# Row-sum reciprocals by block transpose and memory instead of TensorE transposes, and last keys over 128 rows

## The chip, the cores and the metric

One core of a Trainium2 chip. Time is device time in microseconds (us). TensorE (PE) multiplies and writes to PSUM, VectorE (DVE) and ScalarE (ACT) read PSUM and SBUF, GpSimd (POOL) works on SBUF, and SyncE's queue (SP) issues every DMA of this kernel. Each engine takes its own list of instructions in order.

## The reference

Causal attention with a decay for 4 x 8 heads of 576 tokens and 64 dimensions, then a mixture of 8 experts over 2304 tokens with iterated normalization of the gate, then a two-layer network:

```python
cum = np.cumsum(np.log(np.clip(f, 0.0001, 1.0)), axis=-1)
scores = scale * q @ k.T + cum[:, None] - cum[None, :]       # per head, causal
attn = np.exp(scores - scores.max(-1, keepdims=True))
x = attn / (attn.sum(-1, keepdims=True) + 1e-09) @ v
P = np.exp(x @ w_gate - max)                                 # then 8 times:
P /= P.sum(1, keepdims=True); P /= P.sum(0, keepdims=True); P *= N / E
y = sum(P[:, e:e+1] * (np.maximum(x @ w1[e], 0) @ w2[e]) for e in range(8))
out = np.maximum(0.01 * (y @ w_in), y @ w_in) @ w_out
```

## The kernel before

**Attention, 0 to 296 us.** Heads are taken one after another and normalized in pairs (even head n with n + 1). For a head, `qk` computes scores in six pieces x over query blocks of 128, 128, 128, 96 and 96 rows (`QKS`), each as two products (L452, L453); `qk_min` (L464, VectorE) masks them and takes the row minimum of the negated scores; `qk_exp` (L477, ScalarE) exponentiates and sums each row into `st`. `tr` (L504, PE) transposes the exponentials, `tr_hi` (L511, ScalarE) copies them out. In most heads the transposed exponentials and v are split into a high and a low part of reduced precision: `tr_lo` (L520, VectorE) makes the low part `ptl`, `vp` and `vl` those of v, and `pv` (L541, PE) multiplies both. `pv` gives the output transposed, dimensions on partitions, tokens along the row, in two column ranges r of 256 and 320 tokens. Keys come in five blocks, the last of which has 64 keys, so its products contract over 64 rows. The heads in `NATIVE` (0, 1, 2, 4 and 6) are not split; their products run in full precision, which takes PE longer. `pv_copy` (ScalarE) and `pv_add` (L569, VectorE) bring the output into `xs`, 128 partitions for two heads.

**Normalization of a pair.** Row sums lie with tokens on partitions, while the outputs have tokens along the row. `recip` (L583 to L585, VectorE) takes reciprocals in `st`; `spread` (L590, GpSimd) copies each 64 times along the row into `rb`; `norm_t` (L599, PE) transposes the five blocks of `rb` into the PSUM tile `ps_r`, blocks 0 and 1, then 2 to 4; `norm_m` (L605, VectorE) multiplies `xs` by it. Then `x_hi`, `x_lo` split `xs`, `x_store` writes it to memory, `gate` (L650, PE) multiplies it by the gate's weights.

**Fills.** Between these PE runs "fills", products of the first experts (L213: 384 columns, L240: 512 columns), with their weights loaded (`wr`, L143) and split (L154, L158). What attention has not taken of the fills follows behind the gate's logits (L944), over the eight normalizations of the gate, and partly between the first expert products (L1400).

**What sets the order.** `head_events` names each step with its engine, an assumed duration, its needs and a due time (tables `HEAD_T`, `HEAD_E` for native heads, `PAIR_T`, `PAIR_E`; `base_of` gives the pace). `run_heads` simulates the five queues with them and writes each engine's list: the earliest start wins, and a later step with an earlier due time may go first within a bound. Fills go in where PE has nothing due. "VP" marks steps of VectorE that are kept apart from GpSimd's. `run_events` does the same for the expert stages, beginning with the fills that are left.

Of the kernel before, what the change touches and what calls it, by code (L numbers as in the profile page):

```python
# [15 lines left out]
ALU = mybir.AluOpType  # L16
# [36 lines left out]
    qk0=0.082, qk1=0.116, qk2=0.397, qk3=0.562, qk4=0.212, qk5=0.672,  # L53
    t0=1.293, t1=1.192, t2=1.370, t3=0.995, pv0=1.618, pv1=1.989,
# [3 lines left out]
    nt0=3.799, ga0=4.707, nt1=3.866, ga1=4.635,  # L58
# [4 lines left out]
NATIVE = (0, 1, 2, 4, 6)  # L63
# [3 lines left out]
    qk0=-0.150, qk1=-0.138, qk2=0.915, qk3=0.306, qk4=0.749, qk5=0.774,  # L67
    t0=1.579, t1=1.706, t2=1.194, t3=0.921, pv0=1.375, pv1=2.127,
)
PAIR_E = dict(  # L70
    nt0=3.970, ga0=4.804, nt1=3.484, ga1=4.601,
# [17 lines left out]
def moe_kernel(ctx, tc, qT, kT, v, fg, w_gate, w1, w2, w_in, w_out, out):  # L89
# [214 lines left out]
    with ExitStack() as actx:  # L304
# [49 lines left out]
        fone = a1.tile([P, 512], F32, tag="p3", name="fone")[:B * H, 0:S // 2]  # L354
# [10 lines left out]
        ca = a2.tile([P, PTW], F32R, tag="pth", name="pth")[:B * H, 0:2 * S].rearrange(  # L365
# [59 lines left out]

        vps = {}
# [13 lines left out]
        QKS = [(4, 0, 288), (4, 288, 576), (0, 0, 128), (1, 0, 256), (2, 0, 384), (3, 0, 512)]  # L440
# [30 lines left out]
        def qk_exp(n, x):  # L471
            i, k0, k9 = QKS[x]
            m = QT[i][1]
            if (n, i) not in prb:
                prb[n, i] = (a2 if i == 4 else a1).tile([P, QN[i]], F32, tag=f"p{i}", name=f"p{i}")
# [16 lines left out]
        def tr(n, u):  # L492
            if n in NATIVE:
                if n not in pts:
                    pts[n] = (a2.tile([P, PTW], F32, tag="pth", name="pt"),)
            elif n not in pts:
                pts[n] = (a2.tile([P, PTW], F32R, tag="pth", name="pth"),
                          a2.tile([P, PTW], F32R, tag="ptl", name="ptl"))
# [28 lines left out]
        def pv(n, r):  # L527
# [5 lines left out]
            for x, (j, s) in enumerate(todo):  # L533
# [3 lines left out]
                if n in NATIVE:  # L537
                    vp = rvs[(n // 2) % 2][:KV[j], j].rearrange("p h d -> p (h d)")
# [35 lines left out]
        rbs, rps, parts = {}, {}, {}  # L574

        def stat(n):
            stats[n // 2] = a2.tile([P, 3, 5, 2], F32, tag="st", name="st")
            nc.gpsimd.memset(stats[n // 2], 1.0)

        def recip(n):  # L580
# [4 lines left out]
            nc.vector.reciprocal(rs, rs)  # L585

        def spread(n):
            rs = stats[n // 2][:, 0]
            rbs[n] = a1.tile([P, 5, P], F32, tag="rb", name="rb")
            nc.gpsimd.tensor_copy(  # L590
                rbs[n].rearrange("p i (h d) -> p (i h) d", h=2),
                rs.rearrange("p i h -> p (i h)").unsqueeze(2).to_broadcast([P, 10, D]))

        def norm_t(n, r):
            ra, rb = RG[r]
            ps = ps_t.tile([P, 512], F32, tag="t", name="ps_r")
            for i in ((0, 1), (2, 3, 4))[r]:
                q0, m = QT[i]
                nc.tensor.transpose(ps[:, q0 - ra:q0 - ra + m], rbs[n][:m, i, :], ident[:m, :m])  # L599
            rps[n, r] = ps  # L600

        def norm_m(n, r):
            ra, rb = RG[r]
            xs = xss[n // 2]
            nc.vector.tensor_tensor(xs[:, ra:rb], xs[:, ra:rb], rps.pop((n, r))[:, :rb - ra], ALU.mult)  # L605
# [63 lines left out]
        TE, TL = 6.9, 8.6  # L669
# [25 lines left out]
        M_QK = (0.27, 0.27, 0.18, 0.235, 0.36, 0.47)  # L695
        M_TR = (0.41, 0.40, 0.48, 0.16)
        V_MN = (0.40, 0.57, 0.22, 0.35, 0.49, 0.65)
        A_EX = (0.47, 0.47, 0.36, 0.46, 0.57, 0.68)
        A_HI = (0.47, 0.44, 0.50, 0.28)
        V_LO = (0.58, 0.55, 0.62, 0.36)  # L700

# [1201 lines left out]
```

## Time and profile before

| | us |
|---|---|
| median of 3 runs | 2006.63 |
| lowest, highest | 2006.27, 2008.97 |
| profiled execution, its own time | 2007.51 |
| its span, first to last instruction | 2005.6 |

| engine | busy us | share |
|---|---|---|
| PE | 1982.9 | 99% |
| VectorE | 1663.2 | 83% |
| ScalarE | 982.7 | 49% |
| GpSimd | 1039.3 | 52% |

Busy PE is not PE at its peak: matmuls overlap, and their ends are modelled. The distance between the starts of two matmuls in the timeline tells what one costs.

### The profile page before, as it was taken

Reading aid. Unit: us, or ns where it says so; the run is one execution under the profiler, and the core shown is the slowest. Engines: PE = TensorE matmul, PEld = TensorE weight load, DVE = VectorE, ACT = ScalarE, POOL = GpSimd, SP = SyncE. Lnnn points to the kernel's source line nnn. Section 1 sums busy time; section 2 is a strip of 40 time slices with the busy share of each in tenths; the row PEclk is TensorE's granted clock in tenths of the full one; section 3 lists DMA queues with packets and bytes.
Section 4 is the critical chain, followed back from the end, with each engine's and each line's share of the span. In section 5 each row is a group of like instructions: output and inputs, shape, how many; then the busy total and the mean of one; then the engine's idle time right before and its main releaser. Section 6 shows DMA issues by size and latency. Waiting matters only on the chain.

```text
span 2005.6 us, 32286 instructions
## 1 busy us (share of the span) xinstructions
PE 1982.9 (99%) x11600; PEld 1941.2 (97%) x11600; DVE 1663.2 (83%) x2467; ACT 982.7 (49%) x1753; POOL 1039.3 (52%) x732
## 2 busy tenths in 40 slices
PE   7999999999999999999999999999999999999999
PEld 6888888999999999999999999999999999999998
DVE  8988976788888888888888888888888878887766
ACT  7877865454433443444344334434433346655443
POOL 5766655345555555555554555555464563343301
PEclk9999999999999999999999999999999999999999
DMA  5655528578887778776777777677777745776563
GB/s 155 185 151 164 142 88 276 200 287 268 277 275 284 260 239 275 246 250 242 254 247 245 272 243 250 241 258 251 243 269 242 249 181 199 276 248 214 194 204 138
DMA packets 145623, 460.55 MB, mean 230 GB/s; under 512 B 15912, under 2 KB 42168, under 8 KB 145464
## 3 DMA queue, kind: packets, MB, share of 16 engines
q1 hardware_dynamic: 145464, 458.49, 68.1%
q8 instruction: 93, 1.52, 0.3%
q14 instruction: 66, 0.54, 0.1%
HBM read 402.76 MB, written 51.08 MB: 226 GB/s over the span
## 4 chain that ended last, share of the span: by engine, by line
PE 91%; DVE 3%; ACT 2%; DMA 2%; issue 1%; SPq 0%; POOL 0%; DVEq 0%; ACTq 0%
PE x L1400 46%; PE y L1400 34%; PE ps_t L504 1%; PE ps_pv L541 1%; DMA wr<-in_w_dram 1%; PE ps_m L240 1%; PE ps_s L452 1%; PE ps_m L213 1%; PE ps_s L453 1%; ACT p L477 1%; PE ps_m L541 1%; PE y L213 1%; PE x L240 1%; DVE ps_s L464 1%; PE x L213 1%
## 5 line engine op out<-in xcount | busy, mean ns | idle before, releaser
L1400 PE MATMUL x<-xw,w 128*128 128x384 f32 x2676 | 499.9, 334 | 0.0
L1400 PE MATMUL x<-hh,w 128*128 128x384 f32 x1792 | 490.6, 334 | 0.0
L1400 PEld LDWEIGHTS x<-xw,w 128*128 128x128 f32 x2676 | 467.2, 188 | 0.7 <-issue 0.3
L1400 PE MATMUL y<-xw,w 128*128 128x384 f32 x2004 | 374.7, 334 | 0.0
L1400 PE MATMUL y<-hh,w 128*128 128x384 f32 x1344 | 368.0, 334 | 0.2 <-DVE acc_C L1483 0.2
L1400 PEld LDWEIGHTS y<-xw,w 128*128 128x128 f32 x2004 | 349.6, 188 | 0.1
L1222 POOL TENSOR_TENSOR w<-wr,w 128x512 fp32r<-128x512 f32 x163 | 211.0, 1295 | 228.0 <-DVE hl L1471 51.6
L1400 PEld LDWEIGHTS x<-hh,w 128*128 128x128 f32 x1792 | 326.8, 188 | 0.0
L1400 PE MATMUL x<-hl,w 128*128 128x384 f32 x896 | 299.4, 334 | 0.3 <-POOL hl L1471 0.3
L1400 PEld LDWEIGHTS y<-hh,w 128*128 128x128 f32 x1344 | 244.9, 188 | 0.5 <-issue 0.5
L1400 PE MATMUL y<-hl,w 128*128 128x384 f32 x672 | 224.5, 334 | 0.0
L1483 DVE TENSOR_TENSOR acc_C<-x,acc_C 128x768 f32<-128x768 f32 x177 | 168.9, 954 | 55.3 <-PE x L1400 52.5
L1483 DVE TENSOR_TENSOR acc_C<-y,acc_C 128x768 f32<-128x768 f32 x148 | 141.5, 956 | 67.1 <-PE y L1400 65.6
L154 ACT ACTIVATE w<-wr 128x512 fp32r<-128x512 f32 x288 | 175.1, 621 | 32.0 <-PE y L1400 15.9
L1400 PEld LDWEIGHTS x<-hl,w 128*128 128x128 f32 x896 | 168.2, 188 | 0.6 <-POOL hl L1471 0.6
L1467 ACT ACTIVATE hh<-u 128x768 fp32r<-128x768 f32 x91 | 77.1, 847 | 151.6 <-PE y L1400 91.2
L1467 ACT ACTIVATE hh<-k 128x768 fp32r<-128x768 f32 x112 | 94.9, 848 | 100.8 <-PE y L1400 50.7
L1467 ACT ACTIVATE hh<-spare 128x768 fp32r<-128x768 f32 x84 | 71.2, 847 | 142.3 <-PE y L1400 65.0
L1400 PEld LDWEIGHTS y<-hl,w 128*128 128x128 f32 x672 | 126.2, 188 | 0.0
L1467 ACT ACTIVATE hh<-c 128x768 fp32r<-128x768 f32 x70 | 59.3, 847 | 118.0 <-PE y L1400 93.5
L1436 ACT ACTIVATE u<-x 128x768 f32<-128x768 f32 x91 | 74.1, 814 | 86.8 <-PE x L1400 80.2
L1210 POOL TENSOR_TENSOR wr<-wr 128x512 f32<-128x512 f32 x55 | 71.2, 1295 | 84.0 <-DVE wr L1210 32.2
(263 smaller groups left out, 3637.2 us busy)
## 6 DMA issues: line engine op xcount, KB each, us to landing
xw<-xo_t SPq DMA_DIRECT2D x208, 768.0 KB
xw<-xo_b SPq DMA_DIRECT2D x154, 768.0 KB
wr<-in_w_dram SPq DMA_DIRECT2D x88, 512.0 KB
pb<-prow SPq DMA_DIRECT2D x44, 384.0 KB
xo_t<-xw SPq DMA_DIRECT2D x16, 768.0 KB
rq<-in_qT_dram SPq DMA_DIRECT2D x64, 144.0 KB
rk<-in_kT_dram SPq DMA_DIRECT2D x64, 144.0 KB
xo_b<-xw SPq DMA_DIRECT2D x12, 768.0 KB
```

The lines of the kernel that those rows point to most:

```text
L154: nc.scalar.activation(hv, src, AF.Copy)
L213: nc.tensor.matmul(ps, w_[:, fs], x_[k][:, xs], start=(x == 0), stop=(x == 11))
L240: nc.tensor.matmul(ps, h_[:, ts], w_, start=(x == 0), stop=(x == 11))
L452: nc.tensor.matmul(o, q1[:, q0:q0 + m], k1[:, k0:k9], start=True, stop=False)
L453: nc.tensor.matmul(o, q2[0:D + 4, q0:q0 + m], k2[0:D + 4, k0:k9], start=False, stop=True)
L541: nc.tensor.matmul(ps[:, a - ra:rb - ra], vp, s[:KV[j], o:o + rb - a], start=(x == 0), stop=(x == len(todo) - 1))
L1210: ENG[e].tensor_tensor(o, x, y, op)
L1222: ENG[e].tensor_tensor(lo, blk(g, which, WSRC[which][n]), f(hi), ALU.subtract)
L1400: nc.tensor.matmul(o_, w[:, k, w_], m[:, k, :], start=a and k + y == 0, stop=z and k == 1 and y == 2, skip_group_check=True)
L1436: nc.scalar.activation(ctile(u, name, name, bufs), pview(u, p), AF.Copy)
L1467: nc.scalar.activation(hi, tmp[u, LSRC[l]], AF.Copy)
L1483: nc.vector.tensor_tensor(a, pview(u, l), a, ALU.add)
```

## The change

The five reciprocal blocks are no longer spread and transposed on PE. `st` becomes 32 columns wide, of which ten hold the sums; VectorE's block transpose turns it in blocks of 32 x 32 into `turned`; four small DMAs write ten rows each to a DRAM tile `rd`, and two DMAs read it back broadcast over 64 partitions each into `rb`, from where `norm_m` multiplies in SBUF, in ranges of 384 and 192 tokens. Heads 3, 5 and 7 become native. The tiles of transposed exponentials are now fixed ones, whose rows beyond the last 64 keys are cleared once, so that the last keys' products run over 128 rows. The last query block computes 480 score columns instead of 512. Due times and assumed durations change (one line of each is shown).

```diff
-    nt0=3.799, ga0=4.707, nt1=3.866, ga1=4.635,
+    nt0=5.002, ga0=4.901, nt1=3.561, ga1=4.607,
...
-NATIVE = (0, 1, 2, 4, 6)
+NATIVE = (0, 1, 2, 3, 4, 5, 6, 7)
...
+        for t_ in [f(t_) for t_ in pths + ptls] + ptfs:
+            nc.gpsimd.memset(t_[D:, PTOFF[4]:], 0.0)
...
+        nc.gpsimd.memset(p3[:, 480:], 0.0)
...
-        QKS = [(4, 0, 288), (4, 288, 576), (0, 0, 128), (1, 0, 256), (2, 0, 384), (3, 0, 512)]
+        QKS = [(4, 0, 288), (4, 288, 576), (0, 0, 128), (1, 0, 256), (2, 0, 384), (3, 0, 480)]
...
-                    vp = vps[n - n % 2].rearrange("p j (h c) -> p j h c", h=2)[:KV[j], j, n % 2]
+                    vp = vps[n - n % 2].rearrange("p j (h c) -> p j h c", h=2)[:, j, n % 2]
                 nc.tensor.matmul(
-                    ps[:, a - ra:rb - ra], vp, s[:KV[j], o:o + rb - a],
+                    ps[:, a - ra:rb - ra], vp, s[:, o:o + rb - a],
...
             nc.vector.reciprocal(rs, rs)
-
-        def spread(n):
-            rs = stats[n // 2][:, 0]
-            rbs[n] = a1.tile([P, 5, P], F32, tag="rb", name="rb")
-            nc.gpsimd.tensor_copy(
-                rbs[n].rearrange("p i (h d) -> p (i h) d", h=2),
-                rs.rearrange("p i h -> p (i h)").unsqueeze(2).to_broadcast([P, 10, D]))
-
-        def norm_t(n, r):
-            ra, rb = RG[r]
-            ps = ps_t.tile([P, 512], F32, tag="t", name="ps_r")
-            for i in ((0, 1), (2, 3, 4))[r]:
-                q0, m = QT[i]
-                nc.tensor.transpose(ps[:, q0 - ra:q0 - ra + m], rbs[n][:m, i, :], ident[:m, :m])
-            rps[n, r] = ps
+            turned[n] = a2.tile([P, 32], F32, tag="turned", name="turned")
+            nc.vector.transpose(turned[n], stt.pop(n))
+
+        def r_out(n):
+
+            t_ = turned.pop(n)
+            for b in range(4):
+                nc.sync.dma_start(out=rd[n // 2 % 2][:, 32 * b:32 * b + 32], in_=t_[32 * b:32 * b + 10])
+
+        def r_in(n):
+            rbs[n] = a2.tile([P, 5, P], F32, tag="rb", name="rb")
+            src = rd[n // 2 % 2].rearrange("(i h) q -> h i q", h=2)
+            for h in range(2):
+                nc.sync.dma_start(
+                    out=rbs[n][h * D:(h + 1) * D], in_=src[h:h + 1].to_broadcast([D, 5, P]))
...
-            nc.vector.tensor_tensor(xs[:, ra:rb], xs[:, ra:rb], rps.pop((n, r))[:, :rb - ra], ALU.mult)
+            x, r_ = ((xss[n // 2][:, 0:384], rbs[n][:, 0:3]), (xss[n // 2][:, 384:S], rbs[n][:, 3:5, 0:96]))[r]
+            x = x.rearrange("p (i q) -> p i q", q=r_.shape[2])
+            nc.vector.tensor_tensor(x, x, r_, ALU.mult)
...
-        TE, TL = 6.9, 8.6
+        TE, TL = 6.859, 8.418
...
+            hv(("ro", n), ("D", 1.5, 2.0), r_out, n, need=[("rc", n), ("ri", n - 4)])
+            hv(("ri", n), ("D", 0.8, 2.0), r_in, n, need=[("ro", n)] + [("nm", n - 4, r) for r in range(2)])
```

**The order on three engines.** On PE, in the middle of attention, the transposes into `ps_r` stood between output products (`ps_pv`) and fills (`ps_m` from `xp`). Before:

```order
L452 MATMUL ps_s<-k_2151,q_2150 96x512
L453 MATMUL ps_s<-k_1_216,q_1_214 96x512
L213 MATMUL ps_m<-xp,w 128x384 x4
L599 MATMUL ps_r<-ident,rb 128x128 x2
L213 MATMUL ps_m<-xp,w 128x384 x4
L541 MATMUL ps_pv<-pth,vp 128x256
L541 MATMUL ps_pv<-ptl,vp 128x256
L541 MATMUL ps_pv<-pth,vp 128x128
L541 MATMUL ps_pv<-ptl,vp 128x128
L599 MATMUL ps_r<-ident,rb 128x128
L599 MATMUL ps_r<-ident,rb 128x96 x2
L541 MATMUL ps_pv<-pth,vp 128x320
```

The same place on PE in the changed program, with the gate's products (`ps_g`) ahead of the output products:

```order
L661 MATMUL ps_g<-xth,wg 128x384
L213 MATMUL ps_m<-xp,w 128x384 x4
L461 MATMUL ps_s<-k_1952,q_1951 128x256
L462 MATMUL ps_s<-k_0_215,q_0_213 128x256
L660 MATMUL ps_g<-xp,wg 128x192
L661 MATMUL ps_g<-xp,wg 128x192
L461 MATMUL ps_s<-k_1952,q_1951 96x480
L462 MATMUL ps_s<-k_0_215,q_0_213 96x480
L547 MATMUL ps_pv<-pth_231,vp 128x256
L547 MATMUL ps_pv<-ptl_233,vp 128x256
L547 MATMUL ps_pv<-pth_231,vp 128x128
L547 MATMUL ps_pv<-ptl_233,vp 128x128
```

The transposes are gone there and at 15 other pairs. Ahead of the logits PE now has 240 fill products of 384 columns and 180 of 512, before 216 and 144.

On SP, in the early part of attention, between the loads of heads (`rq`, `rk`), the small rows of the decay (`cd`) and a store of `xs`, before:

```order
L687 DMA q_1_214<-cd 2x576
L688 DMA k_1_216<-cd 2x576
L143 DMA wr<-in_w_dram 128x2x512
L325 DMA rq<-in_qT_dram 64x576
L326 DMA rk<-in_kT_dram 64x576
```

The like place on SP in the changed program:

```order
L698 DMA k_1_216<-cd 2x576
L701 DMA q_1_214<-q_1003 64x576
L642 DMA xd_2_102<-xs 128x576
L603 DMA rd_262<-turned 10x32 x4
L143 DMA wr<-in_w_dram 128x2x512 x2
L609 DMA rb<-rd_262 64x5x128 x2
L325 DMA rq<-in_qT_dram 64x576
L326 DMA rk<-in_kT_dram 64x576
```

The write of the reciprocals and the broadcast read stand on SP's list, here with two weight loads between them.

On VectorE, in the middle of attention, the multiplications (`xs` from `xs` and `ps_r`) stood around the next pair's reciprocals, before:

```order
L605 TENSOR_TENSOR xs<-xs,ps_r 128x256
L520 TENSOR_TENSOR ptl<-ps_t,pth 128x512
L434 CAST vp<-rv_193 128x5x2x64
L583 TENSOR_TENSOR st<-st 96x2
L584 TENSOR_SCALAR st<-st 128x10
L585 RECIPROCAL st<-st 128x10
L605 TENSOR_TENSOR xs<-xs,ps_r 128x320
L569 TENSOR_TENSOR xs<-ps_pv,xt 64x256
```

The reciprocals on VectorE in the changed program, with 24 rows left out, and the multiplications of the same pair:

```order
L593 TENSOR_TENSOR st<-st 96x2
L594 TENSOR_SCALAR st<-st 128x10
L595 RECIPROCAL st<-st 128x10
L597 STREAM_TRANSPOSE turned<-st 128x32
...
L526 TENSOR_TENSOR ptl_233<-ps_t,pth_231 128x96
L526 TENSOR_TENSOR ptl_233<-ps_t,pth_231 64x96
L615 TENSOR_TENSOR xs<-xs,rb 128x384
L615 TENSOR_TENSOR xs<-xs,rb 128x192
L409 CAST q_2993<-rq 128x576
L473 ISA ps_s,st<-ps_s,mask 96x288
```

The multiplications stand ahead of the next pair's reciprocals, 27 rows behind the block transpose, and the next heads' work stands directly behind them.

## Rows read from the trace of the kernel before

**Rows 1.** Busy us (instructions) of PE, PEld, DVE, ACT, POOL, clock, DMA, by stretch
```profile
20.00:296.00 276.00, 269.43 (x1769) 237.05 (x1769) 245.53 (x794) 219.15 (x664) 188.06 (x162) 1.00 0.54 148
...
1000.00:1500.00 500.00, 500.00 (x2887) 500.00 (x2886) 429.05 (x494) 199.14 (x282) 276.04 (x182) 1.00 0.74 252
```

**Rows 2.** Timeline of PE in one pair: start us, us, instruction
```profile
130.40 0.28 PE L541 MATMUL ps_pv<-ptl,vp 128*128 128x128 f32 x1
130.51 0.40 PE L599 MATMUL ps_r<-ident,rb 128*128 128x128 f32 x2
130.67 0.48 PE L240 MATMUL ps_m<-w,hh 128*128 128x512 f32 x1
130.98 0.40 PE L240 MATMUL ps_m<-w,hl 128*128 128x512 f32 x1
...
131.68 0.39 PE L452 MATMUL ps_s<-k,q 128*96 128x512 f32 x1
131.91 0.40 PE L453 MATMUL ps_s<-k,q 68*96 68x512 f32 x1
132.15 0.44 PE L599 MATMUL ps_r<-ident,rb 128*128 128x128 f32 x3
132.37 0.39 PE L541 MATMUL ps_pv<-pth,vp 128*128 128x320 f32 x1
132.60 0.31 PE L541 MATMUL ps_pv<-ptl,vp 128*128 128x320 f32 x1
132.75 0.31 PE L541 MATMUL ps_pv<-pth,vp 128*128 128x320 f32 x1
```

**Rows 3.** Timeline of PE at the end of a split head's second output product
```profile
159.72 0.27 PE L541 MATMUL ps_pv<-ptl,vp 128*128 128x192 f32 x1
159.93 0.31 PE L541 MATMUL ps_pv<-pth,vp 64*128 64x96 f32 x1
160.07 0.27 PE L541 MATMUL ps_pv<-ptl,vp 64*128 64x96 f32 x1
160.28 0.37 PE L452 MATMUL ps_s<-k,q 128*96 128x288 f32 x1
```

**Rows 4.** Chain of work, output products: start us, us, what (x10: second range)
```profile
18.20 0.66 PE ps_m L541 x4
19.68 2.36 PE ps_m L541 x10
...
92.53 0.63 PE ps_pv L541 x4
...
132.59 1.46 PE ps_pv L541 x10
```

**Rows 5.** Groups by line, POOL: busy us, mean ns, idle before
```profile
L331 POOL MEMSET rv<- 64x128 f32 x2 | 0.3, 199 | 0.1
```

**Rows 6.** Chain of work, transfers in it: start us, us, what
```profile
8.39 1.72 DMA q<-pth
...
104.41 2.62 DMA rk<-in_kT_dram
...
116.61 8.88 DMA wr<-in_w_dram
...
305.38 4.33 DMA acc_C<-xd
```

**Rows 7.** Timeline of SP's queue, issues: start us, us, what
```profile
148.48 0.23 SPq L687 DMA_DIRECT2D q<-cd  x1
...
149.10 0.47 SPq L325 DMA_DIRECT2D rq<-in_qT_dram  x1
```

**Rows 8.** Timelines of PE, SP and DVE where the expert products begin
```profile
357.78 2.24 PE L1400 MATMUL x<-xu,w 128*128 128x384 f32 x12
...
340.37 0.46 SPq L1338 DMA_DIRECT2D pb<-prow  x1
...
363.14 0.96 DVE L1453 SCALAR_TENSOR_TENSOR k<-y,pb 128x768 f32<-128x768 f32 x1
```

More of the change, by code (lines that the diff above doesn't have):

```diff
@@ L66 @@
 HEAD_E = dict(
-    qk0=-0.150, qk1=-0.138, qk2=0.915, qk3=0.306, qk4=0.749, qk5=0.774,
-    t0=1.579, t1=1.706, t2=1.194, t3=0.921, pv0=1.375, pv1=2.127,
+    qk0=-0.204, qk1=-0.019, qk2=1.586, qk3=0.247, qk4=0.605, qk5=0.848,
+    t0=1.015, t1=1.103, t2=1.211, t3=0.849, pv0=1.310, pv1=1.970,
 )
 PAIR_E = dict(
-    nt0=3.970, ga0=4.804, nt1=3.484, ga1=4.601,
+    nt0=5.007, ga0=4.913, nt1=3.914, ga1=4.352,
 )
@@ L353, in moe_kernel @@
         nc.vector.memset(mx, 0.0)
-        fone = a1.tile([P, 512], F32, tag="p3", name="fone")[:B * H, 0:S // 2]
+        p3 = acst.tile([P, QN[3]], F32, name="p3")
+        fone = p3[:B * H, 0:S // 2]
         nc.vector.memset(fone, 1.0)
@@ L364, in moe_kernel @@
             cum[:, S // 2:], fone, fr[:, S // 2:], cum[:, S // 2 - 1:S // 2], ALU.mult, ALU.add)
-        ca = a2.tile([P, PTW], F32R, tag="pth", name="pth")[:B * H, 0:2 * S].rearrange(
+        pths, ptls = ([acst.tile([P, PTW], F32R, name=f"{n}{i}") for i in range(2)] for n in ("pth", "ptl"))
+        ptfs = [acst.tile([P, PTW], F32, name=f"ptf{i}") for i in range(2)]
+        ca = pths[1][:B * H, 0:2 * S].rearrange(
             "p (j s) -> p j s", j=2)
@@ L492, in tr @@
         def tr(n, u):
[L493 to L498, printed above, removed]
+            if n not in pts:
+                pts[n] = (ptfs[n % 2],) if n in NATIVE else (pths[n % 2], ptls[n % 2])
             ps = ps_m.tile([P, 512], F32, tag="m", name="ps_m") if n < PVM and u in TRM else \
@@ L571, in pv_add @@
                 xts.pop((n, r))[me, 0:rb - ra], ALU.add)
-        rbs, rps, parts = {}, {}, {}
+        rbs, parts = {}, {}
+        stt, turned = {}, {}
+        rd = [dram.tile([10, P], F32, name=f"rd{i}") for i in range(2)]
         def stat(n):
-            stats[n // 2] = a2.tile([P, 3, 5, 2], F32, tag="st", name="st")
-            nc.gpsimd.memset(stats[n // 2], 1.0)
+            stt[n] = a2.tile([P, 32], F32, tag="st", name="st")
+            stats[n // 2] = stt[n][:, :30].rearrange("p (r j h) -> p r j h", r=3, h=2)
+            nc.gpsimd.memset(stt[n], 1.0)
         def recip(n):
@@ L694, in moe_kernel @@
         XI = [4, 4, 0, 1, 2, 3]
-        M_QK = (0.27, 0.27, 0.18, 0.235, 0.36, 0.47)
+        M_QK = (0.27, 0.27, 0.18, 0.235, 0.36, 0.44)
         M_TR = (0.41, 0.40, 0.48, 0.16)
-        V_MN = (0.40, 0.57, 0.22, 0.35, 0.49, 0.65)
-        A_EX = (0.47, 0.47, 0.36, 0.46, 0.57, 0.68)
+        V_MN = (0.40, 0.57, 0.22, 0.35, 0.49, 0.62)
+        A_EX = (0.47, 0.47, 0.36, 0.46, 0.57, 0.65)
         A_HI = (0.47, 0.44, 0.50, 0.28)
@@ L761, in head_events @@
             T = PAIR_E if n in NATIVE else PAIR_T
-            hv(("rc", n), ("VP", 0.5, 0.1), recip, n,
-               need=[("ex", n + y, x) for y in range(2) for x in range(6)])
-            hv(("rb", n), ("P", 0.72, 0.05), spread, n,
-               need=[("rc", n)] + [("nt", n - 2, r) for r in range(2)])
+            hv(("rc", n), ("VP", 0.6, 0.1), recip, n,
+               need=[("ro", n - 4)] + [("ex", n + y, x) for y in range(2) for x in range(6)])
+            hv(("ro", n), ("D", 1.5, 2.0), r_out, n, need=[("rc", n), ("ri", n - 4)])
+            hv(("ri", n), ("D", 0.8, 2.0), r_in, n, need=[("ro", n)] + [("nm", n - 4, r) for r in range(2)])
             for r in range(2):
-                hv(("nt", n, r), ("M", (0.23, 0.3)[r], 0.17), norm_t, n, r, need=[("rb", n)],
-                   ring="t", rel=[("nm", n, r)], due=place(n, T[f"nt{r}"]))
-                hv(("nm", n, r), ("V", (0.35, 0.42)[r], 0.07), norm_m, n, r,
-                   need=[("nt", n, r)] + [("cp" if n + y in NATIVE else "ad", n + y, r) for y in range(2)])
+                hv(("nm", n, r), ("VP", (0.5, 0.28)[r], 0.07), norm_m, n, r,
+                   need=[("ri", n)] + [("cp" if n + y in NATIVE else "ad", n + y, q)
+                                       for y in range(2) for q in range(2)])
             hv(("xs", n), ("A", 0.62, 0.1), x_hi, n, need=[("nm", n, 0), ("nm", n, 1)]
```

17 lines of the change are left out of this document (8 added, 9 removed).

## The prediction

> **What bounds the kernel now.** I read the page's busy table first, then busy time by stretch. From 1000 to 1500 us, in the expert stages, TensorE (PE) is busy for all 500.00 us, so nothing can be won there but products themselves, and the change touches none of those. In the attention stage, 20 to 296 us, PE is busy for 269.43 of 276 us, while VectorE is busy for 245.53 us in 794 instructions, 0.309 us each, and idle for 30.5 us [rows 1]. Attention is therefore close to bound by PE, with VectorE second. Whatever attention leaves over, PE fills with "fill" products of the first experts, which have to be done anyway: the total of PE's work sets the end. A microsecond of PE work removed is a microsecond of the kernel, unless a new wait takes it back.
>
> A duration in a row is not a price. Two transposes last 0.40 us from 130.51 us on, but the next matmul starts 0.16 us later [rows 2]: matmuls overlap, and the price is the distance from one start to the next.
>
> **The change part by part.**
>
> *Transposes of the reciprocals.* Eighty go: five for each of 16 pairs, mostly as a group of two and a group of three. In the timeline of one pair two take 130.51 to 130.67, or 0.16 us, three take 132.15 to 132.37, or 0.22, and the matmul behind each group takes 0.31 and 0.23 until the next start, where its like take 0.23 (131.68) and 0.15 (132.60) [rows 2]: 0.16 + 0.22 + 2 x 0.08 = 0.54 us for a pair, 8.6 us for 16. Bounds: 16 x 0.38 = 6.1 without the slower neighbours, 9.1 if every group costs 0.08 more on its other side for one pair in five.
>
> *Last keys over 128 rows.* In a head with split operands the last three starts of the second output product are 0.21, 0.14 and 0.21 us apart (128x192 low part, then the two with 64 rows) [rows 3], 0.56 together. With all 128 rows, a low part of 128 columns leaves 0.11 to the next start (130.40) [rows 2]; three such are 0.33, and the neighbour behind may be slower by 0.08 too, as behind a transpose. Between 0.23 and 0.31 I take 0.30 us, since the operands here are shorter still; 24 heads give 7.2 us. Bounds: 0 (the gaps could come from short operands instead of 64 rows), and 24 x 0.47 = 11.3, if only columns counted (384 at the 0.23 us of 512 columns, 0.17 of 0.64). The Trainium skill states in "TensorEngine Tiling (Array Packing)", Key Properties, that a change of tiling mode drains the engine; in "TensorE: Matmul & The Clock Gate", Step-by-step, it says that loading time follows columns and that the number of rows does not matter. The second rule alone would give 0 here and is the first rival below; the gaps agree with the first rule.
>
> *Native heads.* Heads 3, 5 and 7 are no longer split. A native head's two output products last 0.66 + 2.36 us in the chain against 0.63 + 1.46 of a split one [rows 4], 0.93 more; less the same 0.30 for the last keys, 0.63 net, three heads: 1.9 us more. The five native heads of before gain about 0.30 each, 1.5 us; the trace merges their ten products, so 0 to 2.3 is open. VectorE loses the low parts, the additions and the value copies of three heads; GpSimd loses three value subtractions and 16 broadcast copies. Both are beside PE; I book nothing.
>
> *480 instead of 512 columns.* One product of 512 columns takes 131.68 to 131.91, 0.23 us [rows 2]; 32 columns of it are 0.0145, times 64 products 0.9 us. VectorE and ScalarE shorten too, booked at nothing.
>
> Removed from PE: 8.6 + 7.2 - 1.9 + 1.5 + 0.9 = 16.3 us (4.2 to 22.2 by the bounds).
>
> *What is added.* VectorE gets one block transpose a pair, which no row shows; at the mean of 0.309 us it is 16 x 0.3 = 5 us beside 30.5 us of idle time, and the normalization itself covers the same 576 columns. POOL clears some strips once at the start; the nearest memset takes 0.199 us [rows 5], eight are 1.6 us, hidden behind the first loads, between 0 and 1.6 if that cover fails. SP issues six more DMAs a pair.
>
> *The new wait.* The reciprocals now travel: four small writes, a landing, two broadcast reads, a landing; then VectorE's two multiplications. VectorE takes its list in order, so behind these wait the next heads' minima, low parts and additions, and ScalarE's exponentials and PE's transposes wait for those. What the trip takes is bounded by rows: four issues like the small one of 0.23 us, a landing like the small 1.72 us, two issues like 0.47 us, a landing of 2.62 us (a 144 KB load) to 4.33 us [rows 6, 7]: 0.9 + 1.7 + 0.9 + 2.6 to 4.3 = 6.1 to 7.8 us, say 7.1. In the order of the changed program the multiplications stand 13 to 45 instructions behind the block transpose (30, 24, 25, 25, 28, 22, 31, 27, 22, 27, 23, 43, 26, 45, 22, 13 for the 16 pairs); at 0.309 us that is 4.0 to 13.9 us. Against 7.1 us the shortfalls are 0.3 in three pairs and 3.1 in the last, 4.0 together; against 6.1 only the last pair's 2.1; against 7.8 they are 8.1. Four pairs have a weight load in front of the broadcast in SP's list, and such a load can take 8.88 us [rows 6]; two of these have 25 and 22 instructions of cover, so I add 2 us. VectorE's idle time absorbs part, since it is 1.9 us a pair; I let 4 of these 6 us reach PE. The Trainium skill, "DMA: Bandwidth & Descriptors", Anatomy of one DMA, gives about 2.0 us fixed plus bytes at 436 GB/s; by that the trip would be an estimated 6.2 us, the loss about 2 and the time 2 us lower. No single row isolates this, so I keep my 4.
>
> *The join to the experts.* By the order, 60 fill products (24 of 384 columns, 36 of 512) move from behind attention into it. That shortens the cover of the gate's normalization. At 0.23 us for 512 columns [rows 2] and 3/4 of that for 384 they are 8.3 + 4.1 = 12.4 us, so the first expert product, now at 357.78 us, should come at about 345. The probabilities it leads to are loaded from 340.37 on and first used at 363.14 [rows 8], 22.8 us later: 10 us remain. Cost nothing, up to 3 us if the load lands in a queue.
>
> **Sum.** 16.3 - 4 = 12.3 us faster. The profiled execution took 2007.51 us (span 2005.6 and 1.9 around it), so 1995.2; it lies 0.9 above the median of 2006.63, to which the forecast belongs: **1994.3 us**.
>
> **Rivals.**
>
> 1. *The last keys cost what they cost.* If the gaps belong to the 96 columns, 7.2 + 1.5 us of the sum stay and the new native heads cost 0.9 us more: 1994.3 + 9.6 = 2003.9. For it: 96-column operands are the shortest of the product. Against: the gap begins at the low part with 192 columns and 128 rows before them, 0.21 us to the next start, and it ends behind the second of the two: it stands at the change of rows, on both sides.
>
> 2. *The trip makes it slower.* Place: VectorE's two multiplications. The broadcast is 320 KB in short rows, larger than the 144 KB load of the rows, and shares its queue with loads of 512 KB. If the trip takes 9.6 us, the shortfalls of the 16 pairs sum to 28 us (0.3, 2.2, 1.9, 1.9, 0.9, 2.8, 0, 1.3, 2.8, 1.3, 2.5, 0, 1.6, 0, 2.8, 5.6); if all reach PE, the time is 2006.6 - 16.3 + 28 = 2018. It decides from about 8.6 us on, where the shortfalls pass 16. For it: landings of 8.88 us occur. Against: VectorE has idle time and PE has fills placed between heads.
>
> 3. *The join is bared.* The stage behind attention has 12.4 us less cover. If SP's list puts the probabilities late, PE waits 5 to 8 us there: about 2001. Against: 10 us of room.
>
> 4. *More is won.* VectorE's relief in heads 3, 5 and 7 (four low parts, two additions each) shortens the first 110 us and the waits cost nothing: 16.3 + 3 = 19, so 1987.
>
> **Numbers.** Forecast 0.60 with its own range 1989 to 1999; rival 1 0.08, rival 2 0.13, rival 3 0.10, rival 4 0.09. A measurement of this kernel tells about 0.2% from no change, 4 us: faster is below 2002.6. Faster: 0.60 + 0.09 + 0.08 of rival 3 + 0.02 of rival 1 = 0.79; within: 0.06 + 0.02 + 0.01 of rival 2 = 0.09; slower: 0.12. The range 1986 to 2005 leaves out rival 2 and a little on the low side.
>
> **What would show it.** Right: no transposes into ps_r on PE; the two starts behind the 192-column low part 0.11 us apart or less; the first expert product at 343 to 348 us with everything behind it shifted by one constant; VectorE idle before the normalization (xs from xs and rb) released by the DMA of rb, under 8 us in total. Wrong: a gap before that multiplication of 2 us or more in most pairs, PE idle in attention more than 6 us above before, or the first expert product waiting for pb or its operands.

## The result: slower, although TensorE has less work

| | median us | lowest to highest | runs |
|---|---|---|---|
| before, beside it on the same chip | 2007.92 | 2006.27 to 2010.67 | 6 |
| after | 2024.89 | 2019.48 to 2031.91 | 6 |

The ratio is 1.0088, with a 95% interval of 1.0068 to 1.0107: slower by 17 us, where 12 us faster were forecast. The profiled execution has a span of 2021.1 us against 2005.6.

The page's busy table of the changed kernel (engine, busy us, share, instructions):

```profile
PE 1976.8 (98%) x11520; PEld 1938.2 (96%) x11520; DVE 1651.6 (82%) x2462; ACT 980.5 (49%) x1753; POOL 1022.1 (51%) x717
```

Busy time by stretch, the columns of [rows 1]. Attention ran to 296 us before and to 324 us now, so both ends are shown:

```profile
20.00:296.00 276.00, 249.09 (x1584) 221.40 (x1583) 221.01 (x728) 204.99 (x624) 167.52 (x140) 0.96 0.61 163
...
20.00:324.00 304.00, 276.13 (x1752) 245.41 (x1750) 241.26 (x789) 222.75 (x673) 177.36 (x147) 0.97 0.57 155
...
1000.00:1500.00 500.00, 500.00 (x2886) 500.00 (x2885) 431.09 (x500) 199.32 (x282) 268.33 (x177) 1.00 0.73 252
```

The expert stages are unchanged, so the loss lies ahead of them. PE's idle time in attention rose from 276 - 269.43 = 6.6 us [rows 1] to 304 - 276.13 = 27.9. That is 21.3 more; PE's busy time over the whole span fell by 1982.9 - 1976.8 = 6.1, and 15.2 is what is left, against 15.5 us between the spans. Some work went, and more than three times as much idle time came. The granted clock, 1.00 before, is a mean of 0.97 here, which says that PE ran part of the stretch at the lower of its two levels, 1.2 GHz; so its busy time holds a loss too, of which more below.

What the engines waited for between 15 and 324 us (us in total, times, longest):

```profile
ACT w L154 <- DMA wr<-in_w_dram: 17.6, 10, 4.0
PE ps_t L510 <- ACT p L487: 15.0, 10, 3.6
DVE xs L615 <- DMA rb<-rd: 14.4, 10, 3.3
...
ACT xth L630 <- DVE xs L615: 5.3, 4, 2.8
...
ACT xp L630 <- DVE xs L615: 4.6, 3, 2.6
...
SPq L603 <- DVE turned L597: 16.8, 8, 8.2
SPq L609 <- DMA rd<-turned: 3.4, 5, 0.9
```

Before the change ScalarE's wait for these weights was (15 to 296 us)

```profile
ACT w L154 <- DMA wr<-in_w_dram: 8.4, 7, 2.4
```

The forecast's wait is there (DVE for rb, 14.4 us; under 8 was set as the sign of being right). PE's longest wait is for ScalarE's probabilities (p), and ScalarE stood longest, apart from its waits for PE, before the first halves of the fills' weights (w from wr), 17.6 us. It stood for VectorE's multiplications too, 5.3 + 4.6 us, so both causes can reach PE through it; the experiments tell them apart. One pair shows how these belong together; the timeline, engine by engine (SP's with the writes of the next pair as well), in the columns of [rows 2] and [rows 7]:

```profile
93.33 2.56 SPq L603 DMA_DIRECT2D rd<-turned  x4
95.98 0.50 SPq L701 DMA_DIRECT2D q<-q  x1
96.58 0.54 SPq L337 DMA_DIRECT2D rv<-in_v_dram  x1
97.17 0.55 SPq L340 DMA_DIRECT2D rv<-in_v_dram  x1
97.81 0.54 SPq L143 DMA_DIRECT2D wr<-in_w_dram  x1
98.52 1.28 SPq L609 DMA_DIRECT2D rb<-rd  x2
...
115.06 1.39 SPq L603 DMA_DIRECT2D rd<-turned  x4
...
102.91 0.63 ACT L154 ACTIVATE w<-wr 128x512 fp32r<-128x512 f32 x1 [2.17 <-DMA wr<-in_w_dram]
103.56 0.66 ACT L487 ACTIVATE p<-ps_s,st 96x480 f32<-96x480 f32 x1
...
104.21 0.83 DVE L615 TENSOR_TENSOR xs<-xs,rb 128x384 f32<-128x384 f32 x2 [2.73 <-DMA rb<-rd]
...
104.36 0.55 PE L510 MATMUL ps_t<-ident,p 96*128 96x96 f32 x4 [1.75 <-ACT p L487]
```

Read it from below. PE waits 1.75 us for p; ScalarE makes p late because it stood 2.17 us before w; the weights were issued at 97.81, behind four writes of the trip that hold SP for 2.56 us, and landed 5.1 us later, beside the trip's reads. VectorE's wait ends only at 104.21. The trip is longer than forecast (93.33 to 104.21 is 10.9 us, not 7.1; four other DMAs that SP issues between writes and reads take 2.5 of it), and two chains come out of it: one to VectorE, and one through SP's queue to ScalarE. From 98.50 to 104.20 us the DMA engines are nearly full (last but one column, 0.94):

```profile
98.50:104.20 5.70, 4.11 (x28) 3.49 (x27) 2.98 (x10) 3.01 (x10) 1.97 (x2) 1.00 0.94 247
```

Shortly behind this wait PE is at work again, but at the lower level of its clock (last but two column, 0.50):

```profile
106.00:108.00 2.00, 2.00 (x10) 2.00 (x11) 2.00 (x7) 1.85 (x5) 2.00 (x3) 0.50 0.67 175
```

### The profile page after: what moved, and what is told of

It is laid out like the page before. It is cut to its first block, busy times and chain, and to the rows that moved or that the text cites. A ratio compares the mean times of both kernels' runs of the same rounds, so it can differ in the third digit from the quotient of the medians.

```text
span 2021.1 us, 32207 instructions
## 1 busy us (share of the span) xinstructions
PE 1976.8 (98%) x11520; PEld 1938.2 (96%) x11520; DVE 1651.6 (82%) x2462; ACT 980.5 (49%) x1753; POOL 1022.1 (51%) x717
## 4 chain that ended last, share of the span: by engine, by line
PE 85%; DVE 1%; DMA 1%; issue 0%; ACT 0%; SPq 0%; POOL 0%; DVEq 0%; POOLq 0%; ACTq 0%
PE x L1409 45%; PE y L1409 34%; PE y L213 1%; PE y L240 1%; PE ps_m L213 1%; PE x L213 1%; PE x L240 1%; DMA wr<-in_w_dram 1%; PE ps_t L510 0%; PE ps_m L240 0%; PE ps_pv L547 0%; DMA spare<-xd 0%; PE ps_s L461 0%; PE ps_s L462 0%; DMA rb<-rd 0%
## 5 line engine op out<-in xcount | busy, mean ns | idle before, releaser
L1231 POOL TENSOR_TENSOR w<-wr,w 128x512 fp32r<-128x512 f32 x154 | 199.8, 1298 | 217.3 <-DVE hl L1480 54.1
L154 ACT ACTIVATE w<-wr 128x512 fp32r<-128x512 f32 x288 | 175.6, 622 | 35.2 <-DMA wr<-in_w_dram 17.6
```

What stands on the lines that cost most here:

```text
L154: nc.scalar.activation(hv, src, AF.Copy)
L1231: ENG[e].tensor_tensor(lo, blk(g, which, WSRC[which][n]), f(hi), ALU.subtract)
```

## Experiments

Theory T, as forecast: the price is VectorE's wait for the reciprocals. Rival S: the price is the six DMAs' passage through SP and the DMA engines. Rival O: the new order (tables of places, three more native heads) costs time. All were timed beside the kernel before, whose medians there were 2007.4 to 2007.9 us. The runs without the reading, without the DMAs, and those with reads alone or writes alone leave out the normalization by the row sums.

| run | median us | ratio to before, 95% |
|---|---|---|
| no reading of the reciprocals | 2020.87 | 1.0075 (1.0048 to 1.0102) |
| no DMAs of the trip | 1999.12 | 0.9963 (0.9949 to 0.9977) |
| old normalization in the new order | 2011.03 | 1.0018 (1.0008 to 1.0027) |
| planner told of a later trip | 2017.12 | 1.0048 (1.0033 to 1.0063) |
| reads alone | 2010.33 | 1.0009 (1.0000 to 1.0019) |
| writes alone | 2006.74 | 0.9994 (0.9984 to 1.0004) |
| last keys alone, order of before | 2004.70 | 0.9984 (0.9975 to 0.9993) |
| five native heads | 2012.40 | 1.0024 (1.0015 to 1.0033) |
| wide reads | 2022.05 | 1.0078 (1.0061 to 1.0095) |
| one write, one read | 2103.24 | 1.0468 (1.0452 to 1.0484) |
| small reads alone | 2003.38 | 0.9978 (0.9968 to 0.9988) |
| writes alone, waiting for nothing | 2003.46 | 0.9982 (0.9972 to 0.9991) |
| one write, two wide reads | 2013.02 | 1.0027 (1.0014 to 1.0041) |
| last keys alone, planner told | 2001.60 | 0.9976 (0.9967 to 0.9986) |
| one write, two wide reads, planner told | 2010.90 | 1.0019 (1.0009 to 1.0029) |

**No reading of the reciprocals.** In `norm_m` the factor is the tile of ones.

```
-            x, r_ = ((xss[n // 2][:, 0:384], rbs[n][:, 0:3]), ...)[r]
+            x, r_ = ((xss[n // 2][:, 0:384], ones.unsqueeze(1).to_broadcast([P, 3, P])), ...)[r]
```

> The changed kernel, with all its DMAs and its order, but the normalization multiplies by the constant tile of ones instead of the reciprocals that come back from memory, so that VectorE waits for no landing (the outputs are not normalized). Theory T (the trip through memory ends in a wait of VectorE ahead of the multiplications, ScalarE's split and PE's transposes wait behind it): 1993 us, between 1989 and 1999. Rival S (the six DMAs of a pair delay the other loads on SP's queue and on the DMA engines): 2015 to 2025, since every DMA is still there. Rival O (the new order and the native heads 3, 5, 7 are slow by themselves): 2015 to 2025.

2020.87 us: the kernel stays slow without VectorE's wait. By the two ratios that wait is worth 2.6 us, uncertain by some 7. T falls as the main cause. ScalarE's wait for the multiplications is down from 9.9 to 1.9 us; what it and PE still wait for here:

```profile
ACT w L154 <- DMA wr<-in_w_dram: 18.0, 8, 4.0
...
PE ps_t L510 <- ACT p L487: 10.9, 6, 3.4
```

**No DMAs of the trip.** The same, without the four writes and two reads; all else and the planner's order stay.

> As the kernel without the read, and the four writes and two broadcast reads of each pair are left out too (outputs are not normalized). T: within 3 us of the kernel without the read, about 1992. S: 1993 here while the kernel without the read stays above 2015. O: 2015 to 2025 in both. The difference of the two is the price of the DMAs themselves.

1999.12 us, 21.8 less than with them. Nothing consumed their data in either run, so passage alone costs 21.8 us, uncertain by some 6: S holds, and O alone, which asked for 2015 to 2025 here, does not. But S asked for 1993: 6 us of the forecast's gain are missing even without a single DMA of the trip. The rows of this run, to be set beside those of the changed kernel above:

```profile
PE 1969.8 (99%) x11520; PEld 1931.4 (97%) x11520; DVE 1650.8 (83%) x2462; ACT 980.4 (49%) x1753; POOL 1022.2 (51%) x717
```
```profile
20.00:296.00 276.00, 264.09 (x1723) 234.98 (x1722) 237.71 (x783) 220.38 (x671) 176.18 (x146) 0.98 0.53 148
```

```profile
ACT w L154 <- DMA wr<-in_w_dram: 9.4, 7, 2.6
...
PE ps_t L510 <- ACT p L487: 3.9, 5, 2.8
```

Against the run without reading, which differs by the DMAs alone, ScalarE's wait for weights falls from 18.0 to 9.4 us (8.4 before the change), and PE's wait for p from 10.9 to 3.9. The chain read in the pair above goes with the DMAs. It is not the whole of the 21.8 us: which other loads carry the rest was not read.

PE's products are the same 11520 in this run and in the changed kernel, and still they keep PE busy for 7.0 us less (1969.8 against 1976.8), at a clock of 0.98 against 0.96 between 20 and 296 us. So of the 22.2 us between the two spans (2021.1 and 1998.9) 15.2 are idle time of PE, and 7.0 are the same work taking longer, which fits the lower clock behind the waits; no run holds the clock fixed.

**Old normalization in the new order.** Copy, transposes on TensorE and PSUM products put back; native heads, tables of the heads, last keys and 480 columns stay new.

> The changed kernel with the old normalization (copies on GpSimd, transposes on PE, multiplication from PSUM) and its old due times; native heads, 128 rows and 480 columns stay, the planner orders it anew. T and S: the parts that are left should win 7.2 + 1.5 + 0.9 - 1.9 = 7.7 us against before, so 1999 to 2001. O: 2010 or more.

2011.03 us, 10 more than T and S expected, and O's end: the new order is worse than that of before for this normalization. So O, which is not the price of the trip, is there beside it.

**Planner told of a later trip.**

```
-            hv(("ro", n), ("D", 1.5, 2.0), r_out, ...)
+            hv(("ro", n), ("D", 1.7, 2.2), r_out, ...)
-            hv(("ri", n), ("D", 0.8, 2.0), r_in, ...)
+            hv(("ri", n), ("D", 1.3, 5.0), r_in, ...)
```

> The changed kernel, but the planner is told that the broadcast lands 5.0 us after 1.3 us of issue instead of 2.0 after 0.8, and the writes 2.2 after 1.7 instead of 2.0 after 1.5, so that it puts the multiplications later on VectorE. T: the waits for rb on VectorE fall from 14.4 us to under 4 and the time to 1995 to 2005. S: no change beyond 5 us, above 2018. O: above 2018.

2017.12 us, 7.8 less than the changed kernel (uncertain by some 5), just below the 2018 of S and O and far from T's 1995 to 2005. VectorE's wait for rb, 14.4 us in the changed kernel, is gone from its list altogether, while ScalarE's wait for weights is still 17.1 us. T's wait is cured and most of the loss stays: placing recovers a part and no more.

**Reads alone, writes alone.** Both from the run without reading. In the first the writes are gone and the rows in memory are written once with ones; in the second the reads are gone.

> The changed kernel in which the normalization multiplies by a constant and the four writes of each pair are gone; the scratch rows in memory are written once at the start with ones, and the two broadcast reads of each pair stay, at their places in SP's order, and have nothing of VectorE to wait for. Left out: the normalization by the row sums. With all six DMAs the kernel takes 2020.9 us, without any 1999.1. If it is the broadcast reads' traffic (12,000 packets more than before) and their issue that delay the loads, this stays at 2015 to 2021. If it is SP standing still for VectorE, with the loads of the next heads and weights behind it in the queue, this falls to 1999 to 2004, and ScalarE's idle time before the weights' first halves (18.0 us with all six) falls to the 8 to 10 us of the kernel without them.

> The changed kernel in which the normalization multiplies by a constant and the two broadcast reads of each pair are gone; the four writes stay at their places in SP's order and wait for the turned reciprocals. Left out: the normalization by the row sums. If SP's standing still for VectorE (16.6 us before these writes with all six) is the cost, this takes 2012 to 2021. If the reads' traffic is, 1999 to 2003. Both ends short of 2021 by about the same would say that they share it, since SP also stands for the first read behind the writes (3.4 us).

2010.33 and 2006.74 us: 11.2 and 7.6 above the run without DMAs; the sum of 18.8 leaves 2.9 for the reads' wait for the rows and other joint effects. Neither end of either expectation was met; they share the cost. (A difference of two such medians is uncertain by some 3 us, one with the first run by 6, so the 2.9 is not told from nothing.)

**Small reads alone; writes that wait for nothing.** Two reduced forms of these. The reads fetch one partition in place of 64; the writes take ones from a constant tile in place of the turned reciprocals.

```
-                    out=rbs[n][h * D:(h + 1) * D], in_=src[h:h + 1].to_broadcast([D, 5, P]))
+                    out=rbs[n][h * D:h * D + 1], in_=src[h:h + 1])
```
```
-                nc.sync.dma_start(out=rd[...][:, 32 * b:32 * b + 32], in_=t_[32 * b:32 * b + 10])
+                nc.sync.dma_start(out=rd[...][:, 32 * b:32 * b + 32], in_=ones[32 * b:32 * b + 10, 0:32])
```

> The run with the reads alone (2010.3 us; no writes, nothing to wait for, normalization by a constant) with each read cut from 64 partitions to one: the same 32 issues on SP at the same places, a sixty-fourth of pieces and bytes. Left out: the normalization by the row sums. Without any of the DMAs the kernel takes 1999.1. If traffic is the cost, 1999 to 2001; if SP's time for issuing (0.6 us each) is, 2007 to 2011.

> The run with the four writes alone (2006.7 us; no reads, normalization by a constant), in which they write ones from a constant tile in place of the turned reciprocals: the same 64 issues and pieces at the same places on SP, and nothing of VectorE to wait for. Left out: the normalization by the row sums. Without any of the DMAs the kernel takes 1999.1. If SP's standing still for VectorE (17.5 us before these writes) is what costs, this takes 1999 to 2002. If the issuing of 64 DMAs does (0.3 us each, 20 us of SP's time), it stays at 2005 to 2008.

2003.38 and 2003.46 us, both between their two ends. Of the reads' 11.2 us, 4.3 stay when 63 of 64 partitions go: that is the price of 32 issues, and 7.0 that of the data. Of the writes' 7.6 us, 4.3 stay when nothing is waited for: the price of 64 issues; 3.3 is that of SP standing still. With 3 us of uncertainty in each, the 7.0 is clear of nothing, the two 4.3 barely, the 3.3 hardly. The waits of the run with waiting writes, and then of the one with free writes:

```profile
SPq L603 <- DVE turned L597: 17.5, 8, 8.2
...
PE ps_t L510 <- ACT p L487: 10.1, 8, 2.4
```
```profile
PE ps_t L510 <- ACT p L487: 5.0, 5, 1.6
```

17.5 us of standing cost 3.3 us of time, as it would if most of it fell where nothing behind in the queue was wanted yet.

**Wide reads.** The whole changed kernel, rows kept head by head, so that a read is 64 pieces of 2560 bytes in place of 320 of 512.

```
-            stats[n // 2] = stt[n][:, :30].rearrange("p (r j h) -> p r j h", r=3, h=2)
+            stats[n // 2] = stt[n][:, :30].rearrange("p (r h j) -> p r j h", r=3, h=2)
...
-            src = rd[n // 2 % 2].rearrange("(i h) q -> h i q", h=2)
+            src = rd[n // 2 % 2].rearrange("(h i) q -> h (i q)", h=2)
...
```

> The changed kernel, whole, with the scratch rows in memory kept head by head: a partition's five rows of reciprocals lie side by side, so that each broadcast read is 64 pieces of 2560 bytes in place of 320 of 512. Number of DMAs, bytes, waits and order are those of the changed kernel. If the 10,000 further pieces of the reads are what costs (reads alone cost 11.2 us), this takes 2010 to 2014 against the 2020 to 2025 of the changed kernel, and a read lands in under 2.5 us. If bytes or the number of DMAs on SP's queue cost, it stays at 2018 to 2025.

2022.05 us, no change that can be told (2.9 us less than the changed kernel, uncertain by some 5) and not the 10 us less that the pieces asked for: their number is not the main price. With the small reads this leaves the bytes as the likelier one. 327,680 for a pair, times 16, are 5.2 MB, moved where the DMA engines are at 0.94 already (above). In attention their mean share rises with the reads from 0.53 (no DMAs, above) to 0.60:

```profile
20.00:296.00 276.00, 257.84 (x1657) 229.75 (x1656) 231.56 (x762) 214.11 (x653) 175.48 (x145) 0.97 0.60 165
```

**One write, one read; one write, two wide reads.** Both start from the run with wide reads: the four writes become one, and in the first of the two runs the two reads as well.

```
+            nc.sync.dma_start(out=rd[n // 2 % 2].rearrange("k (b q) -> b k q", b=4), in_=t_)
```
```
+            nc.sync.dma_start(out=rbs[n].rearrange("p i q -> p (i q)"),
+                              in_=src.unsqueeze(1).to_broadcast([2, D, 5 * P]))
```

> The changed kernel, whole, with rows head by head, the turned tile written in one DMA (128 pieces of 128 bytes) and read back in one broadcast (128 pieces of 2560 bytes): two DMAs for each pair of heads on SP in place of six, 64 fewer in all. Planner and order as in the changed kernel. If both pieces and issues cost: 2002 to 2009. If the issues cost and pieces do not: this falls by 5 us or more below the run with wide reads. If neither, both runs stay at 2018 to 2025, and what remains is the dependence itself: SP waiting for VectorE and for the rows, with the loads behind.

> The changed kernel, whole, with rows head by head and the turned tile written in one DMA in place of four; the two reads stay as in the run with wide reads (2022.1 us). It tells apart the two edits of the run with one write and one read, which took 2103 us. If the single read made that loss and issues on SP have a price: 2012 to 2019. If the single write made it: above 2080. If issues have no price: 2019 to 2024.

2103.24 and 2013.02 us. The first lies outside all that was expected of it; the second is what was expected if the single read made that loss. The single write is worth 9.0 us (2022.05 - 2013.02, uncertain by some 4; single times of the second run lie between 2005.3 and 2017.9). That is more than the 4.3 of all 64 issues: VectorE's wait for rb falls with it too, from 12.2 to 6.2 us in the profiled executions, so the prices of the runs above do not simply add in the whole kernel. Its issue takes 0.59 us, where the four took 1.39 and 2.56 in the pairs above:

```profile
90.36 0.59 SPq L602 DMA_DIRECT2D rd<-turned  x1
```

The single read costs 90 us. In the first run, a pair's read, VectorE's wait for it, PE's wait behind that, and the last five microseconds of the landing:

```profile
88.00 0.55 SPq L608 DMA_DIRECT2D rb<-rd  x1
...
100.05 0.83 DVE L614 TENSOR_TENSOR xs<-xs,rb 128x384 f32<-128x384 f32 x2 [5.22 <-DMA rb<-rd]
...
101.47 1.06 PE L510 MATMUL ps_t<-ident,p 128*128 128x128 f32 x4 [6.82 <-DVE ptl L526]
```
```profile
95.00:100.00 5.00, 0.00 (x0) 0.00 (x0) 0.00 (x0) 1.49 (x6) 0.00 (x0) 0.77 0.28 92
```
```profile
DMA  3599998641111111121111111111111111110110
```

The last row cuts 95 to 100 us in 40 slices: after the first microsecond one or two tenths of the DMA engines are at work. 88.00 to 100.05 is 12.1 us, against 98.52 to 104.21, 5.7 us, for the two reads of the changed kernel. The Trainium skill states in "DMA: Bandwidth & Descriptors", Rules for kernel authors, that an outermost dimension of fewer than 16 confines a DMA to at most as many engines; here it is 2, and the trace agrees with its one or two tenths. This run is T at a higher dose: its total wait of VectorE for rb is

```profile
DVE xs L614 <- DMA rb<-rd: 60.4, 11, 7.3
```

and now it weighs most. The mechanism forecast exists, and the changed kernel is short of the point where it rules. The clock adds to the waits: for the same 11520 products PE is busy for 1997.0 us here and for 1969.2 in the run with two reads, at a granted clock of 0.86 against 0.99 between 20 and 296 us.

**One write, two wide reads, planner told.**

> The run with one write and two wide reads, with the planner told of later landings (write 0.8 and 2.2 us, reads 1.3 and 5.0 us of issue and landing, as the traces show, in place of 1.5 and 2.0, and 0.8 and 2.0). It is the best form of the way through memory that the runs so far give. Told the same, the changed kernel took 2017.1 us in place of 2021 to 2025. If the gains add: 2008 to 2013, and the change would still lose to the kernel before; 2004 or less would need the bytes of the reads to be hidden too.

2010.90 us, within what was expected. The best form tried of the way through memory still loses to the kernel before. But it stands in the new order: the old normalization took 2011.03 us there, the same within some 2.5. So in that order this form of the trip costs what the transposes cost; in the order of before it was not tried.

**Last keys alone, order of before.** The kernel before, with zeros under the last 64 keys, 128 rows in their products and 480 columns; the instructions of all five engines stand in the order of before, with seven more zero fills on GpSimd.

```
-                    vp = vps[...][:KV[j], j, n % 2]
+                    vp = vps[...][:, j, n % 2]
-                    ps[:, a - ra:rb - ra], vp, s[:KV[j], o:o + rb - a],
+                    ps[:, a - ra:rb - ra], vp, s[:, o:o + rb - a],
```

> The kernel before, in its own order on all five engines, with only the last keys' products over 128 rows (zeros under the 64 keys), the last part of the probabilities over 480 columns, and seven more zero fills at the start; the transposes on TensorE, the five native heads, the planner's tables and costs are those of before. The theory that the products' saving is real where the order does not change: 24 heads by 2 products by 0.15 us, five native ones at 0.3 and 0.9 us of columns, 9.6 us less, of which the attention stage's idle time takes none to a third: 1998 to 2001. The rival, that time won on TensorE in attention is lost there again to waits for ScalarE or VectorE: 2004 to 2008.

2004.70 us, 2.9 less than the median beside it, which is the rival's end. The work did go (the page's busy table):

```profile
PE 1975.9 (99%) x11600; PEld 1938.6 (97%) x11600; DVE 1663.2 (83%) x2467; ACT 981.7 (49%) x1753; POOL 1039.7 (52%) x739
```
```profile
20.00:296.00 276.00, 264.99 (x1791) 236.79 (x1789) 245.29 (x796) 220.48 (x669) 190.20 (x164) 0.99 0.53 149
```

PE is busy for 7.0 us less in all, but in attention it is idle for 11.0 us instead of 6.6 [rows 1]: an order made for longer products turns 4.4 of the 7.0 into waits.

**Last keys alone, planner told.** The same with the changed kernel's own durations for the planner, so that it makes a new order from the tables of places of before (one line of four is shown).

```
-((0.65, 2.4) if early else (0.44, 1.5))
+((0.65, 2.2) if early else (0.44, 1.22))
```

> The run with the last keys alone (2004.7 us), in which the planner is told their new durations and those of the 480 columns (1.5 to 1.22 and 2.4 to 2.2 us for a head's second part of products, 0.03 us less for three operations), so that it makes an order of its own from the tables of places of before. If the 4 us of further idle time on TensorE came of an order that was made for longer products: 1999 to 2003. If the chain through ScalarE and VectorE makes them in any order: 2003 to 2007. Worse than 2007 would say that the places in the tables hold for one set of durations only.

2001.60 us, as expected if the order had made the idle time: 6.0 us less than before, and the best kernel here that does the whole computation; it beats both. The gain over the run in the old order, 3.1 us, is itself uncertain by some 2.5. Idle time in attention is 9.4 us, PE is busy for 10.4 us less than before in all, and the clock is back at 1.00:

```profile
PE 1972.5 (99%) x11600; PEld 1935.4 (97%) x11600; DVE 1660.6 (83%) x2467; ACT 980.0 (49%) x1753; POOL 1040.6 (52%) x739
```
```profile
20.00:296.00 276.00, 266.60 (x1805) 238.97 (x1804) 250.04 (x795) 221.14 (x673) 193.87 (x166) 1.00 0.52 149
```

**Five native heads.** The run with the old normalization in the new order, with heads 0, 1, 2, 4, 6 in place of eight.

> The changed kernel with the old normalization (copy, transposes on TensorE, products out of PSUM, 2011.0 us) and, besides, the five native heads 0, 1, 2, 4, 6 of before in place of eight; the tables of places and planner costs stay the new ones. If the three new native heads lose the 10 us, by halves of TensorE's products less and so less work to cover ScalarE's chain, this falls to 1999 to 2003, beside the kernel with the last keys alone. If the new tables do, it stays at 2008 to 2013.

2012.40 against 2011.03 us, with overlapping intervals: the native heads are not it. It has the same heads and the same normalization as the run of 2001.60 us. What is left between the two, 10.8 us, is what the planner goes by: the heads' tables of places, the pace (`TE, TL`), and 0.06 us that it now allows VectorE between steps. These came with the new normalization and were not tried apart from each other, nor was the new normalization tried without them, so what they are worth in the changed kernel stays open.

## Why the forecast was wrong

The forecast was 2024.89 - 1994.3 = 30.6 us too low, and two of its steps make this up. With nothing for the trip it would have been 1990.3; the run without the DMAs took 1999.12, 8.8 more. For the trip it has 4 us; the changed kernel took 25.8 us more than that run, 21.8 above what was booked. The second is the larger and is below as "the new wait", the other is the last point.

*PE's work: about right.* Without the DMAs PE's busy time is 1969.8 us, 13.1 below before, where the forecast's removals sum to 16.3; with them it is only 6.1 below, at the lower clock. *Last keys: right.* After the change the starts that answer to [rows 3] are

```profile
101.12 0.27 PE L547 MATMUL ps_pv<-ptl,vp 128*128 128x192 f32 x1
101.23 0.23 PE L547 MATMUL ps_pv<-pth,vp 128*128 128x96 f32 x1
101.30 0.28 PE L547 MATMUL ps_pv<-ptl,vp 128*128 128x96 f32 x1
101.41 0.37 PE L510 MATMUL ps_t<-ident,p 96*128 96x96 f32 x2
```

0.11, 0.07 and 0.11 apart, 0.29 for 0.56, 0.27 saved where 0.30 were booked. It is not one lucky head: between 100 and 290 us, in the heads whose rows stand apart in the trace, these four starts span 0.55 or 0.56 us before (21 heads) and 0.29 or 0.30 after (19 heads). The columns are the same and the rows are 128 for 64, so rival 1 is dead. Of the two rules of the Trainium skill weighed for it, that of "TensorEngine Tiling (Array Packing)" is the one that the gaps follow.

*Transposes: not contradicted.* Between the old normalization in the new order and no DMAs, 2011.03 and 1999.12, lie 11.9 us, and PE is busy for 1979.9 - 1969.8 = 10.1 us less. Booked were 8.6; the rest includes what VectorE, the planner's order and the clock give, which these runs do not part.

*Three native heads: not told from nothing* (1.9 us were booked). *VectorE's block transposes:* 0.211 us each, 3.4 us in all, where 5 were reckoned; no run takes them alone, so that they are covered is not shown.

*The join: right in size.* Expert products begin 14.5 us later (to be set beside [rows 8]), where the logits that close attention come about 28 us later, at 324 in place of 296 (the first row is that of before):

```profile
296.30 2.30 PE L944 MATMUL lg_ps<-sel,lgT 128*128 128x16 f32 x20
```
```profile
323.90 2.30 PE L953 MATMUL lg_ps<-sel,lgT 128*128 128x16 f32 x20
...
372.23 2.24 PE L1409 MATMUL x<-xu,w 128*128 128x384 f32 x12
```

against 357.78. So about 13 us came back through the moved fills, and 12.4 were reckoned. That product comes at 372 rather than 345 because of attention, not of the join; rival 3 did not happen: PE's longest wait from 324 to 420 us is 0.5 us.

*The new wait: this step failed.* "I let 4 of these 6 us reach PE" priced only what waits for the trip's end on VectorE. That part the runs do not contradict: 2.6 us by the ratios, uncertain by 7. What was missing is the price of the trip on what it passes. The forecast had six issues a pair on SP in its list, and the weight load beside them, but asked only whether the load would delay the broadcast. The runs show the reverse: the trip delays what stands behind and beside it, 21.8 us in all, uncertain by 6. By single runs it is made of the reads' bytes (7.0), the issues of 64 writes (4.3) and of 32 reads (4.3), SP standing for VectorE (3.3), and 2.9 of the two together; the 21.8 are shown, the parts below 7 only roughly. No run issued the trip from another engine's queue, so how much of the issues' price belongs to SP's order stays open. The issues were also taken too short: 0.23 us for a write, from a load of 4.5 KB [rows 7], where four take 1.4 to 2.6 us. The estimate of 6.2 us for the trip, worked out from the Trainium skill's "DMA: Bandwidth & Descriptors", Anatomy of one DMA, is farther off than the forecast's 7.1; that section is on DMAs that GpSimd issues, and here SP issues them. Rival 2, at 2018 us, came nearest in time, but for another reason; its place was VectorE.

*A microsecond of PE's work is one of the kernel: half right, and the second step that failed.* This was the base of the sum. Last keys alone, in the order of before, took 7.0 us from PE's busy time and gave 2.9; with the planner told 10.4 gave 6.0; all the forecast's removals without the DMAs took 13.1 and gave 8.3 (2007.42 - 1999.12). The rest came back as idle time of PE, in attention 11.9 us for 6.6 in the last of these. Why so much of it came back is open; the new order is a candidate, worth 10.8 us with the old normalization, and the forecast booked nothing for it.

## What to carry to other kernels

When a step moves from an engine to memory, price three things: what waits for its end, what stands behind it in the issuing queue, and whose bytes it moves beside. Here the second and third made 21.8 us (uncertain by 6), the first 2.6 (by 7). A kernel whose order was planned by durations needs to be planned anew when they change, before a saving is judged: the plan was worth about 3 us to the last keys, and its new tables cost 10.8 with the old normalization.

## What was not expected of the hardware

Small DMAs show in the kernel's time even where nothing waits for their data: 32 reads of 2.5 KB cost 4.3 us, 64 writes of 1.2 KB 4.3 us, each uncertain by some 3. A broadcast whose outermost dimension is 2 was there 12.1 us after its issue and left all but one or two tenths of the DMA engines idle; the same bytes in two reads took 5.7. While PE stood still from 95 to 100 us in that run the granted clock had a mean of 0.77, and in the changed kernel PE, at work again behind a wait of 1.75 us, had 0.50 from 106 to 108. A wait of PE can so be paid twice: the same products kept PE busy for 7.0 us longer in the changed kernel than in the run without the DMAs.
